# Opening the main attention's buffers at the end of the leading attention, with decoding level with it in the queues

## The chip, the cores and the metric

The kernel runs on one core of one Trainium2 chip. Its time is the device time of an execution in microseconds (us), and the median of several executions is compared. The engines are TensorE (PE), ScalarE (ACT), VectorE (DVE), GpSimd (POOL) and SyncE (SP), which here issues every transfer. Each takes its instructions strictly in the order in which the program was written down, and waits for the semaphores of the others.

## The reference

Attention with a top-32 mask, then a gated MLP, then a mixture of eight experts whose weights P come from a softmax that is normalised over tokens and experts in turn:

```python
scores = scale * np.matmul(q, k.transpose(0, 1, 3, 2))          # q, k, v: (4, 8, 576, 64)
kth = np.partition(scores, -top_k, axis=-1)[..., -top_k:-top_k + 1]
scores = np.where(scores >= kth, scores, -1000000000.0)
attn = np.exp(scores - np.max(scores, axis=-1, keepdims=True))
attn = attn / (np.sum(attn, axis=-1, keepdims=True) + 1e-09)
x = np.matmul(attn, v)                                          # to (2304, 512), heads side by side
h = x @ w_in                                                    # (512, 2048)
x = (h * np.cos(h)) @ w_out                                     # (2048, 512)
P = np.exp(x @ w_gate - (x @ w_gate).max())                     # (2304, 8)
for _ in range(8):
    P /= P.sum(1, keepdims=True) + 1e-09
    P /= P.sum(0, keepdims=True) + 1e-09
    P *= N / E
for e in range(E):
    out += P[:, e:e + 1] * (np.maximum(x @ w1[e], 0.0) @ w2[e]) # (512, 1024), (1024, 512)
```

The weights w_in and w_out reach the kernel as 64-bit floats. They are turned into 32-bit floats on the chip, which the kernel calls decoding.

## The kernel before

There are 18 tiles of 128 tokens. Three of them lead: `attention_tile` does their attention head by head in plain fp32 (24 head tiles, the leading attention, class "first attention"), and `moe1_tile_a` and `moe1_tile_b` their MLP ("first mlp"), so that the first three tiles of x are there early. From them `fill` can compute expert products (L373 to L375), which keep TensorE busy while the rest of the attention ("attention", the main attention, L448 and L449 for QK) and of the MLP runs. The fill begins when the last x2fh and x2fl of the third leading tile are written.

Every head tile of either attention runs through `att_tile`: QK in two halves of 288 columns (L452 plain, L448 and L449 split into two parts), copies to sc (L458), four MAX8 and three MATCH_REPLACE8 on VectorE for the 32 largest (L460 to L464), two small steps on GpSimd (L465, L469) around two ScalarE passes (L466, L467), a reciprocal (L470), the scaling on GpSimd (L471), five transposes (L476), and a product with v (AV: L531 leading, L502 and L504 main). The leading tiles end with a copy to x_f (L535).

Decoding works through 32 blocks of 128x512 numbers, 16 of w_in and 16 of w_out. Each block has a 512 KB load to d_raw, one VectorE operation (L326), four on ScalarE (L327 to L330), GpSimd's L331, VectorE's L332, GpSimd's L333 and L334, and a 256 KB store to win_d or wout_d in DRAM. The buffers d_raw, d_mag, d_sgn (four each) and d_low (five) are of the pool "dec". The leading MLP loads its weights back from there, 512 KB at a time, to the four buffers wp, 48 times, for L632 (first product) and L657 (second). The gate between them is L591 and L592 on GpSimd, L593 and L598 on VectorE, L594 and L595 on ScalarE, and eight transposes (L641).

What sets the order is the class `Plan`. Every operation is recorded with an engine, an assumed cost and its dependencies; `issue` then plays the engines forward in time and, whenever an engine is free, gives it the operation with the lowest (rank, number of recording) among those that are ready. The ranks are the table `PRIORITY`, a row for each engine and a column for each of the five classes. The order found so is written down, and the hardware follows it whatever the real times are. Decoding is recorded before everything else, so that at equal rank it goes ahead of the leading attention.

Pools of buffers share memory by time: a pool with `after` opens when the pools named there are done, and each operation that touches it depends on all operations that touched those. The main attention's buffers (kh, kl, qs, qt, vs, ath, atl) are of the pool "att", which opens after "dec"; the fill's (whi, wlo, gh, gl, xh, xl) are of "fl", which opens after "first". The leading attention's kp, vp, qp and at_f are of "first", beside the x_f, wp and gT of the leading MLP.

Of the kernel before, what the change touches and what calls it, by code (L numbers as in the profile page):

```python
# [10 lines left out]
F32 = mybir.dt.float32  # L11
# [7 lines left out]
DRAM = bass.MemoryType.DRAM  # L19
# [7 lines left out]

CLASSES = ("first attention", "first mlp", "decode", "attention", "mlp")
PRIORITY = {
    "PE": (0, 1, 9, 2, 3),  # L30
    "ACT": (0, 0.5, 1, 2, 1.5),
    "DVE": (1, 0, 0.5, 2, 0),
    "POOL": (0, 0.5, 1, 1.5, 2),
    "SP": (0, 1, 0.5, 2, 3),
}


# [34 lines left out]
class Plan:  # L72
# [15 lines left out]
    def buf(self, pool, shape, dtype, name):  # L88
        return Buf(self, pool, shape, dtype, name)
# [141 lines left out]
def fused_kernel(tc, kq, vv, w_in, w_out, w_gate, w1, w2, out, B=4):  # L231
# [3 lines left out]
    nc = tc.nc  # L235
    V, A_, G_, T_ = nc.vector, nc.scalar, nc.gpsimd, nc.tensor
    H, S, D = 8, 576, 64
# [11 lines left out]
    wide = w_in.dtype == mybir.dt.int64  # L249

    pl = Plan(tc, {
        "dram": dict(space=DRAM), "cst": {}, "mlp": {}, "m1": {}, "ph1": {}, "att": dict(after=("dec",)),
        "ph2": dict(after=("att", "ph1")),
        "first": dict(side="right"), "dec": dict(side="right"), "fl": dict(side="right", after=("first",)),
        "psum": dict(space=PSUM),
    })
    for p in ("dram", "cst", "mlp", "m1", "ph1", "psum", "first", "dec"):
        pl.open(p)
    add, buf = pl.add, pl.buf

# [42 lines left out]
    def ring_of(pool, n, shape, dtype, name):  # L303
        return Cycle([buf(pool, shape, dtype, f"{name}{i}") for i in range(n)])
# [100 lines left out]
    wk_r = ring_of("ph1", 2, [128, S], F32, "wk")  # L405
    ex_r = ring_of("ph1", 3, [128, S], F32, "ex")
    m_r = ring_of("ph1", 4, [128, 40], F32, "m")
    kp_r = ring_of("first", 2, [64, 2, S], F32, "kp")
    vp_r = ring_of("first", 2, [128, 2, 5, D], F32, "vp")
    qp_r = ring_of("first", 2, [64, H, 128], F32, "qp")  # L410
    at_r = ring_of("first", 2, [128, 5, 128], F32, "at_f")
    xf_r = ring_of("first", 2, [128, 4, 128], F32, "x_f")
    wp_r = ring_of("first", 4, [128, 2, 512], F32, "wp")
    gT_r = ring_of("first", 2, [128, NF1, 128], F32, "gT")
# [683 lines left out]
```

## Time and profile before

| | us |
|---|---|
| median of 3 runs | 2428.88 |
| the runs | 2426.16 to 2429.28 |
| the profiled execution | 2435.11 |
| its span, first to last instruction | 2433.3 |
| TensorE busy in the span | 2344.6 (96%) |
| VectorE busy | 1835.7 (75%) |
| ScalarE busy | 1370.4 (56%) |
| GpSimd busy | 1285.8 (53%) |

The page of the profile gives busy shares of the whole span, in which stages with quite different limits are mixed. The views used below look closer: the stretches give busy time by engine in a window, the lines of one source line its count with its first and last start, the timeline single instructions in order of time, with the idle time just before one and what ended it in brackets. In a timeline a row can hold several equal instructions ("x4"), and the time is then from the start of the first to the end of the last. Instructions overlap a little with the next, so the price of one in a dense stretch is the distance from its start to the start of the next.

### The profile page before, as it was taken

The page shows a single profiled execution, that of the slowest core. Times are in us where ns is not written, and L with a number is a line of the kernel's source. Part 1 is how long each engine was busy: PE and PEld are TensorE (multiplying, and loading weights), DVE is VectorE, ACT ScalarE, POOL GpSimd, SP SyncE. Part 2 cuts the span into 40 slices and gives each one's busy share as a digit, 9 for nine tenths or more (in the row PEclk, how much of TensorE's full clock was granted, in tenths as well). Part 3 has the DMA queues.
Part 4 walks back from the last instruction along what each step waited for, and adds up shares of the span by engine and source line. Part 5 has one row for each costly group of instructions (what it writes and reads, how often), then busy time and mean ns, then how long its engine had stood idle before and what let it go on. Part 6 is the DMA issues. An engine that isn't in the chain of part 4 may idle for free.

```text
span 2433.3 us, 33804 instructions
## 1 busy us (share of the span) xinstructions
PE 2344.6 (96%) x11161; PEld 1909.7 (78%) x11161; DVE 1835.7 (75%) x3371; ACT 1370.4 (56%) x2754; POOL 1285.8 (53%) x1352
## 2 busy tenths in 40 slices
PE   7885899999999999999999999999999999999999
PEld 3442489888877888888888898888888888888887
DVE  8883599999997999998156887876667666666555
ACT  7885488888888777777366766322222232222221
POOL 6768388779888666665421045433333344444440
PEclk9887999999999999999999999999999999999999
DMA  8656654555533334333344333122222221111101
GB/s 273 205 163 219 215 179 147 150 163 182 150 99 100 96 117 121 120 99 108 113 131 115 96 111 103 42 75 83 74 74 74 74 63 42 41 38 35 35 22 48
DMA packets 162449, 267.44 MB, mean 110 GB/s; under 512 B 15392, under 2 KB 62576, under 8 KB 162272
## 3 DMA queue, kind: packets, MB, share of 16 engines
q1 hardware_dynamic: 162272, 265.27, 36.1%
q8 instruction: 88, 1.44, 0.3%
q14 instruction: 89, 0.73, 0.1%
HBM read 233.34 MB, written 31.87 MB: 109 GB/s over the span
## 4 chain that ended last, share of the span: by engine, by line
PE 77%; DVE 10%; POOL 5%; ACT 3%; DMA 3%; issue 2%; SPq 0%; POOLq 0%; ACTq 0%; DVEq 0%
PE y L373 11%; PE y L374 11%; PE y L375 11%; PE g L375 3%; PE g L374 3%; PE g L373 3%; PE t L476 2%; DVE wk L463 2%; PE h L373 2%; PE h L374 2%; PE h L375 2%; DVE m L464 2%; PE t L502 1%; PE y L385 1%; PE y L384 1%
## 5 line engine op out<-in xcount | busy, mean ns | idle before, releaser
L348 POOL TENSOR_TENSOR wlo<-raw,whi 128x512 fp32r<-128x512 f32 x336 | 448.6, 1340 | 144.6 <-ACT whi L346 110.2
L464 DVE MAX8 m<-wk 128x8 f32<-128x576 f32 x432 | 317.4, 748 | 2.8
L956 DVE SCALAR_TENSOR_TENSOR acc<-y,P,acc 128x512 f32<-128x512 f32 x308 | 228.6, 747 | 99.6 <-PE y L375 99.4
L346 ACT ACTIVATE whi<-raw 128x512 fp32r<-128x512 f32 x416 | 258.4, 626 | 64.4 <-PE y L375 25.4
L463 DVE MATCH_REPLACE8 wk<-m,wk 128x576 f32<-128x576 f32 x288 | 213.9, 743 | 1.8
L373 PE MATMUL y<-whi,gh 128*128 128x512 f32 x448 | 182.6, 408 | 0.0
L375 PE MATMUL y<-whi,gl 128*128 128x512 f32 x448 | 176.4, 394 | 0.0
L373 PE MATMUL y<-gh,xh 128*128 128x512 f32 x450 | 176.2, 392 | 0.1
L374 PE MATMUL y<-wlo,gh 128*128 128x512 f32 x448 | 175.9, 393 | 0.0
L374 PE MATMUL y<-gl,xh 128*128 128x512 f32 x450 | 175.6, 390 | 0.0
L375 PE MATMUL y<-gh,xl 128*128 128x512 f32 x450 | 175.5, 390 | 0.0
L476 PE MATMUL t<-ident,ex 128*128 128x128 f32 (+1 forms) x720 | 133.9, 286 | 22.8 <-ACT at_f L480 6.8
L476 PEld LDWEIGHTS t<-ident,ex 128*128 128x128 f32 (+1 forms) x720 | 87.8, 140 | 72.3 <-issue 14.5
L458 ACT ACTIVATE sc<-s 128x288 f32<-128x288 f32 x288 | 116.5, 405 | 26.0 <-PE s L449 12.9
L471 POOL TENSOR_SCALAR ex<-ex,m 128x576 f32<-128x576 f32 x144 | 110.4, 767 | 39.2 <-DVE m L470 32.6
L466 ACT ACTIVATE ex<-sc,m 128x576 f32<-128x576 f32 x144 | 111.0, 771 | 33.1 <-DVE m L464 32.9
L494 ACT ACTIVATE ath<-t 64x128 fp32r<-64x128 f32 (+3 forms) x272 | 104.5, 395 | 31.3 <-PE t L476 29.1
L460 DVE MAX8 m<-sc 128x8 f32<-128x576 f32 x144 | 107.2, 745 | 17.8 <-ACT sc L458 17.8
L467 ACT ACTIVATE ex<-ex,m 128x576 f32<-128x576 f32 x144 | 111.2, 772 | 5.5 <-POOL m L465 2.3
L463 DVE MATCH_REPLACE8 wk<-m,sc 128x576 f32<-128x576 f32 x144 | 106.7, 741 | 0.2
L373 PEld LDWEIGHTS y<-gh,xh 128*128 128x128 f32 x450 | 84.5, 188 | 19.0 <-DVE acc L952 0.7
L373 PE MATMUL y<-gh,gh 128*128 128x512 f32 x254 | 99.3, 391 | 0.0
(376 smaller groups left out, 7096.2 us busy)
## 6 DMA issues: line engine op xcount, KB each, us to landing
raw<-in_w_dram SPq DMA_DIRECT2D x384, 256.0 KB, 2.6
kq<-in_kq_dram SPq DMA_DIRECT2D x40, 576.0 KB, 4.2
raw<-win_d SPq DMA_DIRECT2D x64, 256.0 KB, 3.0
raw<-wout_d SPq DMA_DIRECT2D x64, 256.0 KB, 2.7
y_d<-st SPq DMA_DIRECT2D x56, 256.0 KB, 3.1
raw<-y_d SPq DMA_DIRECT2D x56, 256.0 KB, 2.7
wp<-win_d SPq DMA_DIRECT2D x24, 512.0 KB, 4.6
wp<-wout_d SPq DMA_DIRECT2D x24, 512.0 KB, 4.4
```

The lines of the kernel that those rows point to most:

```text
L346: put("ACT", act_ns(n), lambda: A_.activation(hv(), rv(), AF.Copy), [rb], [hb])
L348: put(e, c, lambda: f.tensor_tensor(lv(), rv(), hv().bitcast(F32), op=ALU.subtract), [rb, hb], [lb])
L373: T_.matmul(o(), ah(), bh(), start=start, stop=False)
L374: T_.matmul(o(), ah(), bl(), start=False, stop=False)
L375: T_.matmul(o(), al(), bh(), start=False, stop=stop)
L458: put("ACT", act_ns(288, psum=True), lambda c=c: A_.activation(sc.ap[:, c], o(), AF.Copy), [ps_s], [(sc, c.start, c.stop)])
L463: put("DVE", 669, lambda r=r, src=src: V.match_replace(wk.ap, mc(8 * r, 8), src.ap, LOWEST), [src, (m, 8 * r, 8 * r + 8)], [wk])
L464: put("DVE", 669, lambda r=r: V.max(mc(8 * r + 8, 8), wk.ap), [wk], [(m, 8 * r + 8, 8 * r + 16)])
L466: put("ACT", act_ns(S, ap=True), lambda: A_.activation(ex.ap, sc.ap, AF.Prelu, scale=-1.0, bias=mc(31), alpha=TINY), [sc, (m, 24, 32)], [ex])
L467: put("ACT", act_ns(S, ap=True) + 93.0, lambda: A_.activation(ex.ap, ex.ap, AF.Exp, scale=-0.125 / TINY, bias=mc(32), accum_out=mc(33)), [ ...
L476: T_.transpose(pt()[:p, c - c0, :], ex.ap[:, c * 128 : c * 128 + p], ident.ap)
L956: put("DVE", 663, lambda y=y, av=av, pcol=pcol: V.scalar_tensor_tensor(av(), y.ap, pcol(), av(), op0=ALU.mult, op1=ALU.add), [y, P, a], [a])
```

## The change

The ranks of decoding become 0 on ScalarE (1 before), VectorE (0.5 before) and SP (0.5 before), so that it goes ahead of the leading attention on all three. Main attention's rank on TensorE goes from 2 to 0.5, ahead of the leading MLP (1) and still behind the leading attention (0). The leading attention's buffers kp, vp, qp and at_f move to a pool of their own, "lead", and the pool "att" opens after "lead" instead of after "dec". The pool "fl" now waits for "dec" as well as for "first". The scratch for DMA descriptors is made smaller, which leaves room for both "att" and "dec".

```diff
 CLASSES = ("first attention", "first mlp", "decode", "attention", "mlp")
 PRIORITY = {
-    "PE": (0, 1, 9, 2, 3),
-    "ACT": (0, 0.5, 1, 2, 1.5),
-    "DVE": (1, 0, 0.5, 2, 0),
+    "PE": (0, 1, 9, 0.5, 3),
+    "ACT": (0, 0.5, 0, 2, 1.5),
+    "DVE": (1, 0, 0, 2, 0),
     "POOL": (0, 0.5, 1, 1.5, 2),
-    "SP": (0, 1, 0.5, 2, 3),
+    "SP": (0, 1, 0, 2, 3),
 }
...
-        "dram": dict(space=DRAM), "cst": {}, "mlp": {}, "m1": {}, "ph1": {}, "att": dict(after=("dec",)),
+        "dram": dict(space=DRAM), "cst": {}, "mlp": {}, "m1": {}, "ph1": {}, "lead": {}, "att": dict(after=("lead",)),
         "ph2": dict(after=("att", "ph1")),
-        "first": dict(side="right"), "dec": dict(side="right"), "fl": dict(side="right", after=("first",)),
+        "first": dict(side="right"), "dec": dict(side="right"), "fl": dict(side="right", after=("dec", "first")),
...
-    for p in ("dram", "cst", "mlp", "m1", "ph1", "psum", "first", "dec"):
+    for p in ("dram", "cst", "mlp", "m1", "ph1", "lead", "psum", "first", "dec"):
...
-    kp_r = ring_of("first", 2, [64, 2, S], F32, "kp")
-    vp_r = ring_of("first", 2, [128, 2, 5, D], F32, "vp")
-    qp_r = ring_of("first", 2, [64, H, 128], F32, "qp")
-    at_r = ring_of("first", 2, [128, 5, 128], F32, "at_f")
+    kp_r = ring_of("lead", 2, [64, 2, S], F32, "kp")
+    vp_r = ring_of("lead", 2, [128, 2, 5, D], F32, "vp")
+    qp_r = ring_of("lead", 2, [64, H, 128], F32, "qp")
+    at_r = ring_of("lead", 2, [128, 5, 128], F32, "at_f")
...
-    nc = bacc.Bacc("TRN2", target_bir_lowering=False, num_devices=1)
+    nc = bacc.Bacc("TRN2", target_bir_lowering=False, num_devices=1, dynamic_dma_scratch_size=1024)
```

Three places show what this does to the queues. The first is the head of SP's queue. Before:

```order
L267 DMA qp_87<-in_kq_dram 64x8x128
L267 DMA kp_95<-in_kq_dram 64x2x576
L267 DMA vp_97<-in_v_dram 128x2x320
L267 DMA kp_99<-in_kq_dram 64x2x576
L267 DMA vp_101<-in_v_dram 128x2x320
L267 DMA qp_103<-in_kq_dram 64x8x128
L267 DMA d_raw_105<-in_w_in_dram 128x1024
L267 DMA d_raw_109<-in_w_in_dram 128x1024
```

and after:

```order
L267 DMA d_raw_90<-in_w_in_dram 128x1024
L267 DMA d_raw_98<-in_w_in_dram 128x1024
L267 DMA d_raw_100<-in_w_in_dram 128x1024
L267 DMA d_raw_102<-in_w_in_dram 128x1024
L267 DMA qp_104<-in_kq_dram 64x8x128
L267 DMA kp_106<-in_kq_dram 64x2x576
L267 DMA vp_108<-in_v_dram 128x2x320
L267 DMA kp_114<-in_kq_dram 64x2x576
```

The first four loads of raw weights have moved from behind the leading attention's first six loads to ahead of them.

The second place is GpSimd's queue around the last block of decoding. Before, L471 of the last leading tile lies eleven blocks further up, and the last block is followed by the splitting of k and q for the main attention:

```order
L334 TENSOR_TENSOR d_low_275<-d_mag_158,d_low_275 128x512
L333 TENSOR_TENSOR d_low_148<-d_low_148,d_sgn_184 128x512
L331 TENSOR_TENSOR d_mag_181<-d_mag_181,d_sgn_221 128x512
L334 TENSOR_TENSOR d_low_148<-d_mag_171,d_low_148 128x512
L333 TENSOR_TENSOR d_low_169<-d_low_169,d_sgn_221 128x512
L334 TENSOR_TENSOR d_low_169<-d_mag_181,d_low_169 128x512
L348 TENSOR_TENSOR kl_1446<-kq_117,kh_1441 128x576
L432 TENSOR_TENSOR qs_1444<-kq_117,qs_1444 64x128
```

After, the last block stands between the thirteenth and the fourteenth leading tile (L465, L469 and L471 are one tile's three steps):

```order
L469 TENSOR_SCALAR m_199<-m_199 128x1
L334 TENSOR_TENSOR d_low_191<-d_mag_122,d_low_191 128x512
L471 TENSOR_SCALAR ex_249<-ex_249,m_199 128x576
L333 TENSOR_TENSOR d_low_116<-d_low_116,d_sgn_149 128x512
L331 TENSOR_TENSOR d_mag_147<-d_mag_147,d_sgn_169 128x512
L334 TENSOR_TENSOR d_low_116<-d_mag_136,d_low_116 128x512
L333 TENSOR_TENSOR d_low_132<-d_low_132,d_sgn_169 128x512
L465 TENSOR_SCALAR m_225<-m_225 128x1
L334 TENSOR_TENSOR d_low_132<-d_mag_147,d_low_132 128x512
L469 TENSOR_SCALAR m_225<-m_225 128x1
L471 TENSOR_SCALAR ex_322<-ex_322,m_225 128x576
L465 TENSOR_SCALAR m_247<-m_247 128x1
```

The whole of decoding has moved ahead of eleven of the 24 leading tiles.

The third place is TensorE's queue behind the last AV of the leading attention. Before:

```order
L531 MATMUL t<-at_f_301,vp_101 64x128 x5
L657 MATMUL y_1137<-wp_435,gT_753 128x512 x2
L657 MATMUL y_1137<-wp_515,gT_753 128x512 x2
L657 MATMUL y_1137<-wp_307,gT_753 128x512 x2
L632 MATMUL h<-wp_307,x_f_285 128x512
L657 MATMUL y_1137<-wp_369,gT_753 128x512 x2
```

and after, behind the logits (L605, L606) of the first leading tile:

```order
L632 MATMUL h<-wp_298,x_f_354 128x512
L632 MATMUL y_426<-wp_329,x_f_354 128x512 x2
L448 MATMUL s<-kh_1458,qs_1465 128x288
L449 MATMUL s<-kl_1467,qs_1465 128x288
L632 MATMUL y_426<-wp_386,x_f_354 128x512
L448 MATMUL s<-kh_1458,qs_1465 128x288
L449 MATMUL s<-kl_1467,qs_1465 128x288
```

The second product of the first leading tile (L657 with its gT) is done there already, and main attention's first QK follows the last AV closely. From that AV to the first L373, before has 20 QK matmuls of main attention, 14 transposes and no AV of it, and after has 52, 30 and 18; of the 48 first-MLP matmuls of each kind there remain 16 of L632 and 44 of L657 before, and 13 and 32 after.

## Rows read from the trace of the kernel before

**Rows 1.** Stretches: window, length, busy us (instructions) of PE, PEld, DVE, ACT, POOL; PEclk, DMA share, GB/s.

```profile
0.00:100.00 100.00, 79.71 (x234) 39.85 (x234) 84.64 (x175) 75.64 (x157) 70.85 (x84) 0.93 0.81 251
100.00:200.00 100.00, 82.11 (x324) 45.45 (x323) 77.33 (x161) 90.03 (x177) 67.50 (x76) 0.81 0.56 171
200.00:300.00 100.00, 73.51 (x220) 33.92 (x218) 40.49 (x64) 45.04 (x87) 53.53 (x55) 0.92 0.67 224
...
900.00:1000.00 100.00, 99.78 (x522) 83.09 (x521) 98.23 (x219) 77.17 (x176) 64.04 (x84) 1.00 0.39 116
```

**Rows 2.** Stretches of 20 us, the one behind the leading attention.

```profile
200.00:220.00 20.00, 11.31 (x18) 3.87 (x16) 8.64 (x10) 13.19 (x21) 18.11 (x15) 0.69 0.60 207
```

**Rows 3.** Single lines: duration in ns (min/median/max), first and last start in us, form.

```profile
L535 ACT ACTIVATE x_f<-t x24: 254/268/279, 32.3 to 202.7; 64x128 f32<-64x128 f32 x24
L334 POOL TENSOR_TENSOR d_low<-d_mag,d_low x32: 1257/1268/2298, 19.3 to 231.6; 128x512 f32<-128x512 f32 x32
L332 DVE TENSOR_SCALAR d_sgn<-d_mag x32: 403/787/1486, 17.1 to 228.7; 128x512 int32<-128x512 int32 x32
L373 PE MATMUL g<-x2fh,whi x16: 333/337/420, 298.2 to 337.2; 128*128 128x384 f32 x16
```

**Rows 4.** Timeline of POOL in the decoding tail: start us, us, instruction, idle before.

```profile
209.52 1.38 POOL L333 TENSOR_TENSOR d_low<-d_low,d_sgn 128x512 f32<-128x512 f32 x1 [0.36 <-DVE d_sgn L332]
210.86 1.26 POOL L331 TENSOR_TENSOR d_mag<-d_mag,d_sgn 128x512 f32<-128x512 f32 x1
212.09 1.26 POOL L334 TENSOR_TENSOR d_low<-d_mag,d_low 128x512 f32<-128x512 f32 x1
213.78 1.31 POOL L333 TENSOR_TENSOR d_low<-d_low,d_sgn 128x512 f32<-128x512 f32 x1 [0.43 <-DVE d_sgn L332]
```

**Rows 5.** Timeline of DVE at the same time.

```profile
212.16 1.48 DVE L332 TENSOR_SCALAR d_sgn<-d_mag 128x512 int32<-128x512 int32 x1 [2.38 <-POOL d_mag L331]
```

**Rows 6.** Lines of POOL, first 300 us: count, busy us, mean ns, idle before.

```profile
L471 POOL TENSOR_SCALAR ex<-ex,m 128x576 f32<-128x576 f32 x27 | 21.7, 803 | 5.5 <-DVE m L470 4.9 <-PE t L531 0.5
...
L469 POOL TENSOR_SCALAR m<-m 128x1 f32<-128x1 f32 x27 | 8.0, 297 | 29.0 <-ACT ex L467 27.6
L592 POOL TENSOR_SCALAR rr<-tt 128x1024 f32<-128x1024 f32 x6 | 6.6, 1096 | 0.5
```

**Rows 7.** Timeline of DVE in a dense stretch of the leading attention.

```profile
34.63 0.08 DVE L463 MATCH_VALUE_LOAD wk<-m,wk 128x8 f32 x1
...
35.36 1.41 DVE L464 MAX8 m<-wk 128x8 f32<-128x576 f32 x2
36.69 0.91 DVE L332 TENSOR_SCALAR d_sgn<-d_mag 128x512 int32<-128x512 int32 x1
```

**Rows 8.** Timeline of PE, leading attention and first MLP together, at full clock.

```profile
138.39 0.75 PE L452 MATMUL s<-kp,qp 64*128 64x288 f32 x2
139.06 1.13 PE L632 MATMUL h<-wp,x_f 128*128 128x512 f32 x2
140.03 0.60 PE L476 MATMUL t<-ident,ex 128*128 128x128 f32 x4
140.47 1.02 PE L632 MATMUL h<-wp,x_f 128*128 128x512 f32 x2
...
143.19 1.45 PE L531 MATMUL t<-at_f,vp 128*64 128x128 f32 x10
...
169.18 1.13 PE L657 MATMUL y<-wp,gT 128*128 128x512 f32 x2
```

**Rows 9.** Timeline of PE between the end of decoding and the fill.

```profile
266.21 5.32 PE L657 MATMUL y<-wp,gT 128*128 128x512 f32 x12
...
276.72 0.30 PE L448 MATMUL s<-kh,qt 128*128 128x288 f32 x1
276.85 0.29 PE L449 MATMUL s<-kl,qt 128*128 128x288 f32 x1
```

**Rows 10.** PE's waits in the first 300 us: in total, times, longest.

```profile
PE y L657 <- DMA wp<-wout_d: 15.4, 6, 6.4
```

## The prediction

> **What bounds the kernel now.** I read the stretches first, then the start of the kernel queue by queue. In the first three hundreds of microseconds TensorE idles 20.3, 17.9 and 26.5 us, 65 us in all, and its granted clock is below full there; later it is full, as between 900 and 1000 us [rows 1]. So TensorE is the engine that the end waits for, and the change is priced in one place: the time F at which the expert fill begins on TensorE (its first matmul at 298.2 us [rows 3]), and how much main attention TensorE has done by then. A microsecond off F, or a microsecond of attention done before F, is a microsecond off the end.
>
> Three things end before F. The leading attention ends at A = 203 us, with the last x_f; decoding ends at D = 233 us, with the last L334 [rows 3]. Then the rest of the first MLP and the opening tiles of main attention take 65 us. Between A and D the kernel does little but decode: TensorE is busy 11.3 of 20 us at 0.69 of its clock, VectorE 8.6 of 20 [rows 2]. There GpSimd's three passes over a block are the chain, and L333 to L333 is 4.26 us [rows 4].
>
> **The change part by part.** What moves is decoding, to the front of SP, ScalarE and VectorE, and main attention, which may open at A and not at D.
>
> *Decoding.* On GpSimd the order now puts all 32 blocks ahead of the fourteenth leading tile; before, all 24 tiles stood ahead of the last block. GpSimd's own work up to there is 32 blocks at 4.26 us [rows 4], 136 us; 13 leading tiles with L471 at 0.80 us, L469 at 0.30 and L465, taken like L469, some 1.4 us each, 18 us; and two pairs of gate steps (L591, L592) at 1.1 us an operation, 4 us [rows 6]. The first block can't reach GpSimd before its load and its activations; before, the first L334 began at 19.3 us behind six other transfers [rows 3], now the load leads, and I take 10 us. Together D = 10 + 136 + 18 + 4 = 168, taken as 170 us: 63 us earlier. The bounds: with no gap between GpSimd's passes (1.23 us each from start to start [rows 4], 3.7 a block) D is 150; with a VectorE that is late each time it is 186, worked out under the rivals.
>
> VectorE has room for this. A leading tile costs it four MAX8 and three MATCH_REPLACE8: 1.33 us for two MAX8, 0.73 for a replace with its load [rows 7], 4.9 us in all with the reciprocal. Up to D it has 13.5 tiles, 66 us, and 64 decode operations at 0.40 us at best and 0.79 in the median of L332 [rows 3], at most 50 us in that measure: 116 of 160 us. ScalarE was busy 166 of the first 200 us [rows 1] with 24 leading tiles and most of the decoding; up to D it has 12 tiles and all the decoding, so it isn't the limit either. What is given up is the leading attention: 14 tiles by 170 us instead of about 19 (the 24 copies to x_f start between 32.3 and 202.7 [rows 3]). On SP four 512 KB loads of raw weights stand ahead of the first q, k and v. That delays the first leading tile by a few microseconds, which cost nothing while GpSimd sets the pace; without that cover they would be paid in full.
>
> *From D to F.* Now TensorE and VectorE are scarce. From the fourteenth AV to F the new order gives TensorE: 13 QK halves at 0.67 us (start to start), 10 AVs at 1.45, 50 transposes at 0.11 (four of them 0.44) [rows 8]; 28 matmuls of L632 and 48 of L657, each two instructions, at 0.88 (5.32 us for twelve instructions), and 52 QK matmuls of main attention at 0.13 [rows 9]; 30 more transposes, 18 AV matmuls and some 70 small ones at about 0.1. That is 8.7 + 14.5 + 5.5 + 66.9 + 6.8 + 3.3 + 2.3 + 7 = 115 us. VectorE has 10.5 leading and about 7.5 main tiles at 4.9 us, 88 us, and four gates beside them: close behind, not ahead. How dense can TensorE run with such a mix? Between 138.4 and 169.2 us it ran leading tiles and first-MLP matmuls together (the first of 122 instructions and the one after the last stand in [rows 8]): 4 AVs, 8 QK halves, 30 MLP instructions, 20 transposes and 16 of the gate are 28 us of work in 30.8, or 0.92. I take that: 115 / 0.92 = 125 us, and 3 us from GpSimd's last block to the fourteenth AV. F = 170 + 3 + 125 = 298 us, where it was before: what decoding gives, the later leading attention takes.
>
> *What F then holds.* Main attention is further on at F: 52 QK matmuls instead of 20, 30 transposes instead of 14, 18 AV matmuls instead of none. At the same prices that is 4.2 + 1.8 + 2.3 = 8 us of TensorE's time, and it is taken out of a stretch where TensorE is full.
>
> *The rest.* Against the fill, main attention keeps its rank on TensorE; only against the first MLP is the rank turned round, and that is in the order counted above. The smaller scratch for DMA touches no transfer of this profile, all of which SP issues; I cost it at nothing. The fill's buffers now wait for the end of decoding too, which is long past when they open.
>
> **The sum.** 0 + 8 = 8 us off. The profiled execution had a span of 2433.3 and 2435.1 us in all, 6.2 above the median of the runs, 2428.9. So the span becomes about 2425 and the median 2421 us, 0.3% less.
>
> **The rivals.** *About even.* The same order, but TensorE at 0.87 between D and F, because VectorE is loaded to 0.8 beside it and all queues are strictly in order. The stretch takes 132 us, F is 305, and 8 - 7 = 1 us remains: 2428. Anything from 0.84 to 0.90 ends within 5 us of no change. For it speaks that two engines are so full at once; against it the 0.92 that the trace shows.
>
> *Slower: VectorE and GpSimd lock each other.* A decode TENSOR_SCALAR that starts while GpSimd is in a pass takes as long as the pass: 1.48 us beside the L334 that started 0.07 us earlier [rows 4, 5], against 0.40 alone [rows 3]. With GpSimd busy nearly all the time, each of the 64 may meet a pass. At 1.48 us they cost 95 us; with 66 for the tiles VectorE has 161 in a phase of 160, and GpSimd in turn waits for d_sgn. At 0.92 of that, D is 10 + 161 / 0.92 = 185, F is 185 + 128 = 313, 15 us later, less the 8: 7 us slower, 2436. It decides once the mean of L326 and L332 passes 1.2 us. The Trainium skill, "SBUF — State Buffer", section "Who interferes with whom", says that a VectorE instruction in a two-port mode and a GpSimd one exclude each other for the whole instruction, and that whoever issues first wins. By that rule the whole price is due each time GpSimd is ahead; the trace agrees in the 1.48 us, and the median of 0.79 shows that over the whole decoding it was due only part of the time.
>
> *Slower: the wp stream.* All loads go through SP in order, and in the new order the last wp loads stand behind loads of kq, which wait for GpSimd's kl, and behind stores of x_d, which wait for VectorE. If these hold TensorE once more as long as its six waits for wp did before, 15.4 us [rows 10], F is 313 and the kernel again 7 us slower, 2436.
>
> *Not what it says.* If main attention never waited for D but for other engines, opening it earlier brings nothing and the reordering is neutral: 2429. The engines stood idle, not loaded, between A and D [rows 2], so I give this little.
>
> **How the numbers follow.** Forecast 0.42, even 0.26, locked engines 0.20, the wp stream 0.08, not what it says 0.04. A measurement of this kernel can tell some 0.2% (5 us) from no change. So faster 0.42, same 0.30, slower 0.28. The forecast's own range is 2406 to 2424. The whole range takes in D from 158 to 186 and a density of 0.82 to 0.96: with D = 158 and 0.96 F is 281 and the gain 25; with 186 and 0.87 F is 321 and the loss 15. That is 2404 to 2444.
>
> **What would show it.** Right: the last L334 ends near 170 us, the last x_f near 235, the first L373 between 290 and 302; TensorE nearly without idle time from 170 us on, and the stretches from 800 us on as before. The locked engines show as L326 and L332 with means above 1.2 us and a last L334 past 182; the wp stream as waits of L657 of 15 us after the last x_f; the even case as a TensorE that works at under 0.9 between D and F with neither. The forecast is wrong if decoding ends on time and F is still past 305, or if the stretch from F to 800 us, which I take as unchanged, moves by more than 5 us.

## The result and the profile after

The changed kernel takes 2444.5 us (median of 4 executions, 2444.3 to 2447.3) against 2428.7 (2426.2 to 2429.3): ratio 1.0061, 95% interval 1.0041 to 1.0081. It is 15.8 us slower. The forecast was 2421 us, faster; the direction is wrong, and the time lies half a microsecond above the range. The profiled execution of after has a span of 2442.5 us and took 2444.3, its median; that of before lies 6 us above its own, so between the two profiles only 9 of the 16 us can be seen.

The stretches of after that answer to [rows 1], with the columns explained there, and the one from 700 to 800 us:

```profile
0.00:100.00 100.00, 49.55 (x121) 24.27 (x121) 67.76 (x126) 75.43 (x143) 81.91 (x83) 0.86 0.87 274
100.00:200.00 100.00, 83.91 (x262) 42.63 (x260) 88.77 (x160) 72.15 (x143) 72.76 (x76) 0.71 0.49 151
200.00:300.00 100.00, 97.90 (x408) 52.27 (x408) 70.74 (x147) 72.89 (x153) 41.58 (x63) 1.00 0.69 223
...
700.00:800.00 100.00, 85.56 (x390) 68.47 (x389) 83.20 (x122) 81.29 (x135) 77.11 (x66) 0.97 0.29 82
```

The first 100 us hold 49.6 us of TensorE work where they held 79.7; from 200 to 300 us TensorE is now full at full clock, where it worked 73.5. The work has moved behind decoding. The single lines that answer to [rows 3], and VectorE's other decode line:

```profile
L535 ACT ACTIVATE x_f<-t x24: 252/269/272, 50.3 to 250.1; 64x128 f32<-64x128 f32 x24
L334 POOL TENSOR_TENSOR d_low<-d_mag,d_low x32: 1262/1272/1710, 12.8 to 172.3; 128x512 f32<-128x512 f32 x32
L332 DVE TENSOR_SCALAR d_sgn<-d_mag x32: 407/746/1503, 9.7 to 168.8; 128x512 int32<-128x512 int32 x32
L326 DVE TENSOR_SCALAR d_mag<-d_raw x32: 408/520/1496, 4.6 to 150.3; 128x512 int32<-128x512 int32 x32
L373 PE MATMUL g<-x2fh,whi x16: 336/338/522, 314.0 to 351.9; 128*128 128x384 f32 x16
```

Decoding ends at D = 173.5 us (before 232.8), the leading attention at A = 250.3 (202.9), and the fill begins at F = 314.0 (298.2). What TensorE waits for in the first 100 us of after (in total, times, longest):

```profile
PE s L452 <- ACT sc L458: 16.6, 12, 3.2
PE s L452 <- DMA kp<-in_kq_dram: 11.9, 1, 11.9
PE t L476 <- POOL ex L471: 10.8, 3, 4.8
```

and the same of before:

```profile
PE s L452 <- DMA kp<-in_kq_dram: 6.3, 1, 6.3
PE s L452 <- ACT sc L458: 5.5, 7, 1.3
...
PE t L476 <- POOL ex L471: 2.4, 2, 2.2
```

TensorE waits longer for ScalarE's copies, for GpSimd's L471 and for the first loads. (On GpSimd the ranks are as before; decoding has moved ahead of the leading tiles on ScalarE, VectorE and SP.) The first x_f is written at 50.5 us, before at 32.5. In return the waits for wp of [rows 10] are gone: no wait of L657 for wp is left between 200 and 325 us.

**A count that explains the time.** I add up what TensorE loses: its idle time, and half of its busy time where the granted clock is 0.5, the lower of its two levels. (Ahead of the first clock record, some 59 us in before and 69 in after, I take the lower level, since the pairs of L452 show 1.32 us there and 0.75 at the higher one.) Such a pair in before:

```profile
25.65 1.32 PE L452 MATMUL s<-kp,qp 64*128 64x288 f32 x2
```

Span less loss is 2288 to 2295 us in all sixteen profiles here that run the reference's work and no more, whose spans lie between 2416 and 2446 us. So the loss is most of the difference between them; between before and after it grows by 13.4 us and the span by 9.2. Loss up to a time, in us:

```
                        100 us  200 us   at F   behind F   F      work done at F
before                   48.5    81.1   113.7     26.1    298.2       184.5
after                    74.6   117.0   123.2     30.0    314.0       190.9
first 16 blocks ahead    70.9    94.9   102.1     22.9    294.9       192.9
last 16 blocks ahead     48.5    93.3   106.6     21.2    301.9       195.3
```

(The two last kernels are experiments below.) Before loses 33 us between 200 us and F, in the tail of decoding and behind it; after loses 6 there. But by 200 us it has lost 36 more. The change trades a loss behind the leading attention for a larger one during decoding: 36 us more ahead of 200 us against 27 less between there and F.

### The profile page after: what moved, and what is told of

It reads as the page before. It is cut to its first block, busy times and chain, and to the rows that moved or that the text cites. A ratio compares the mean times of both kernels' runs of the same rounds, so it can differ in the third digit from the quotient of the medians.

```text
span 2442.5 us, 33847 instructions
## 1 busy us (share of the span) xinstructions
PE 2347.7 (96%) x11161; PEld 1914.4 (78%) x11161; DVE 1850.1 (76%) x3371; ACT 1377.6 (56%) x2756; POOL 1286.5 (53%) x1352
## 4 chain that ended last, share of the span: by engine, by line
PE 83%; DVE 8%; POOL 4%; ACT 2%; DMA 2%; issue 1%; POOLq 0%; DVEq 0%; ACTq 0%
PE y L373 11%; PE y L375 11%; PE y L374 11%; PE g L373 4%; PE g L374 4%; PE g L375 4%; PE t L476 3%; PE h L373 3%; PE h L374 3%; PE h L375 3%; DVE wk L463 2%; PE t L502 2%; PE y L388 1%; DVE m L464 1%; PE y L384 1%
## 5 line engine op out<-in xcount | busy, mean ns | idle before, releaser
L464 DVE MAX8 m<-wk 128x8 f32<-128x576 f32 x432 | 317.9, 749 | 3.5
L373 PE MATMUL y<-whi,gh 128*128 128x512 f32 x448 | 181.8, 406 | 0.0
L373 PE MATMUL y<-gh,xh 128*128 128x512 f32 x450 | 176.1, 391 | 0.1
L476 PE MATMUL t<-ident,ex 128*128 128x128 f32 (+1 forms) x720 | 134.7, 287 | 32.4 <-POOL ex L471 13.3
L458 ACT ACTIVATE sc<-s 128x288 f32<-128x288 f32 x288 | 116.5, 404 | 29.4 <-PE s L449 15.7
L471 POOL TENSOR_SCALAR ex<-ex,m 128x576 f32<-128x576 f32 x144 | 110.8, 770 | 38.3 <-DVE m L470 35.0
L466 ACT ACTIVATE ex<-sc,m 128x576 f32<-128x576 f32 x144 | 110.9, 771 | 20.9 <-DVE m L464 20.7
L460 DVE MAX8 m<-sc 128x8 f32<-128x576 f32 x144 | 107.6, 747 | 12.9 <-ACT sc L458 12.7
L373 PEld LDWEIGHTS y<-gh,xh 128*128 128x128 f32 x450 | 84.5, 188 | 19.1 <-DVE acc L952 0.8
L373 PE MATMUL y<-gh,gh 128*128 128x512 f32 x254 | 99.2, 391 | 0.0
```

The costliest lines, as they stand in the source:

```text
L373: T_.matmul(o(), ah(), bh(), start=start, stop=False)
L458: put("ACT", act_ns(288, psum=True), lambda c=c: A_.activation(sc.ap[:, c], o(), AF.Copy), [ps_s], [(sc, c.start, c.stop)])
L464: put("DVE", 669, lambda r=r: V.max(mc(8 * r + 8, 8), wk.ap), [wk], [(m, 8 * r + 8, 8 * r + 16)])
L466: put("ACT", act_ns(S, ap=True), lambda: A_.activation(ex.ap, sc.ap, AF.Prelu, scale=-1.0, bias=mc(31), alpha=TINY), [sc, (m, 24, 32)], [ex])
L476: T_.transpose(pt()[:p, c - c0, :], ex.ap[:, c * 128 : c * 128 + p], ident.ap)
```

## The experiments

The times are medians; ratios are to the kernel before on the same chip, with their 95% intervals. D, A, F and the losses come from the profiled execution of each, which lies up to 8 us above the median of its kernel (the last row; 6 in before), so a few microseconds of loss between two rows mean little.

```
                                   median   ratio (interval)          D    A    F   loss to F  behind F
decoding's ranks alone             2435.9  1.0027 (1.0015 to 1.0039)  176  251  300   121.4     25.0
all but decoding's ranks           2427.8  1.0000 (0.9987 to 1.0014)  227  196  310   107.5     24.3
pools and scratch alone            2429.5  1.0013 (0.9999 to 1.0027)  229  198  296   109.4     24.8
attention's TensorE rank back      2444.0  1.0063 (1.0045 to 1.0082)  173  254  305   126.3     27.9
ScalarE's rank back                2442.0  1.0058 (1.0039 to 1.0077)  234  217  325   122.9     28.4
VectorE's rank back                2444.3  1.0076 (1.0051 to 1.0101)  176  253  316   125.1     26.2
transfer queue's rank back         2446.6  1.0083 (1.0062 to 1.0104)  184  254  320   130.4     24.7
before, once more                  2429.1  1.0008 (0.9996 to 1.0019)  233  203  298   112.4     25.9
first 16 blocks ahead              2420.5  0.9967 (0.9954 to 0.9981)  196  232  295   102.1     22.9
last 16 blocks ahead               2418.0  0.9964 (0.9949 to 0.9979)  217  227  302   106.6     21.2
last 8 blocks ahead                2441.5  1.0051 (1.0034 to 1.0067)  229  204  322   117.9     32.3
last 24 blocks ahead               2432.3  1.0017 (1.0004 to 1.0031)  201  243  308   116.0     28.9
first 8 blocks ahead               2421.3  0.9965 (0.9950 to 0.9980)  226  211  303   104.5     27.6
last 16 ahead, pools of before     2417.0  0.9945 (0.9928 to 0.9961)  223  233  287   108.5     23.4
```

### Ranks or pools

Theory 1 was that decoding's ranks starve the leading attention; theory 2 that the cost is in main attention's earlier opening and its rank. Decoding's ranks alone, in the kernel before:

```diff
-    "ACT": (0, 0.5, 1, 2, 1.5),
-    "DVE": (1, 0, 0.5, 2, 0),
+    "ACT": (0, 0.5, 0, 2, 1.5),
+    "DVE": (1, 0, 0, 2, 0),
-    "SP": (0, 1, 0.5, 2, 3),
+    "SP": (0, 1, 0, 2, 3),
```

> The kernel before with only the three decoding ranks of the change (ScalarE, VectorE and the transfer queue at 0); pools, attention's TensorE rank and scratch as before. Theory 1 (decoding's rank starves the leading attention, which then has to be done by a TensorE at its lower clock and as the bound): last decoding tile near 173 us, last x_f 235 to 255 instead of 203, first fill matmul 305 to 315 instead of 298, time 2436 to 2446 us. Theory 2 (the early opening of main attention's buffers and its TensorE rank 0.5 cost the time): last decoding tile near 173, first fill matmul at or before 298, time 2420 to 2430.

The time met theory 1 at its low end, but F stayed at 300: only 3 of the 26 main QK halves that after has done by F are done here. The changed kernel with these three rows put back, everything else as changed:

```diff
-    "ACT": (0, 0.5, 0, 2, 1.5),
-    "DVE": (1, 0, 0, 2, 0),
+    "ACT": (0, 0.5, 1, 2, 1.5),
+    "DVE": (1, 0, 0.5, 2, 0),
-    "SP": (0, 1, 0, 2, 3),
+    "SP": (0, 1, 0.5, 2, 3),
```

> The changed kernel with the three decoding ranks put back (ScalarE 1, VectorE 0.5, queue 0.5); the lead pool, the opening of main attention's buffers at its end, rank 0.5 of attention on TensorE and the scratch stay. Theory 1: last decoding tile near 233, last x_f near 203, main attention starts near 205 on engines that would idle, first fill matmul 293 to 300 with more of main attention done ahead of it than before; time 2412 to 2428 us. Theory 2: the time stays with the change, 2438 to 2446.

D and A came as theory 1 said, and the time is that of before, at the end of what it allowed; F was missed (310), because far more of main attention now stands ahead of it. With attention's TensorE rank back too:

```diff
-    "PE": (0, 1, 9, 0.5, 3),
+    "PE": (0, 1, 9, 2, 3),
```

> As the run without the decoding ranks, and attention's TensorE rank back at 2 too: only the pools and the scratch are changed. Theory 1: within 5 us of the run without the ranks, 2412 to 2430 us. Theory 2, if the cost is in the rank 0.5: 2425 to 2430; if in the early opening: 2438 to 2446.

This time lies in the ranges of both theories; it is the run before that speaks against theory 2.

And the changed kernel with that one row put back, decoding's ranks as changed:

> The changed kernel with attention's TensorE rank put back to 2; decoding ranks and pools as changed. Theory 1: last x_f and first fill matmul stay late (245 to 255, 305 to 316), time 2436 to 2447 us. Theory 2, if the cost is that main attention goes ahead of the first MLP on TensorE: first fill matmul 290 to 302, time 2420 to 2430.

Theory 1 is met, with A at 254, F at 305 and 2444.0 us. Rank 0.5 on TensorE moves F by 9 to 14 us and the time by less than can be told. So the pools alone cost nothing measurable (1.0013), decoding's ranks alone 7.7 us, both together 15.8. The ranks carry the cost; that it doubles with the pools is not explained by these four. The count only places the other 8 us: 5 of them are lost ahead of F and 3 behind it (146.4 us in all with the ranks alone, 154.2 with ranks and pools).

### One rank at a time

Each of the next three is the changed kernel with one of decoding's ranks put back:

```diff
-    "ACT": (0, 0.5, 0, 2, 1.5),
+    "ACT": (0, 0.5, 1, 2, 1.5),
```

> The changed kernel with ScalarE's rank for decoding put back to 1 (VectorE and transfer queue stay at 0, pools as changed). If ScalarE's rank is what starves the leading attention: last decoding tile 195 to 235 us, last x_f 203 to 220, time 2425 to 2434 us. If another of the three does it: last x_f 240 to 255, time 2440 to 2447.

```diff
-    "DVE": (1, 0, 0, 2, 0),
+    "DVE": (1, 0, 0.5, 2, 0),
```

> The changed kernel with VectorE's rank for decoding put back to 0.5 (the others stay at 0). The leading attention has rank 1 there either way, so only the first MLP and the later MLP work change places with decoding: last x_f 245 to 254 and 2440 to 2447 us if ScalarE's or the queue's rank is the cause; 2425 to 2434 if VectorE's is.

```diff
-    "SP": (0, 1, 0, 2, 3),
+    "SP": (0, 1, 0.5, 2, 3),
```

> The changed kernel with the transfer queue's rank for decoding put back to 0.5 (ScalarE and VectorE stay at 0). The leading tiles' loads then go ahead of decoding's again: first leading QK matmul near 6.3 us instead of 11.9. If the queue starves the leading attention: last x_f 203 to 225, time 2425 to 2434 us. If ScalarE's rank does: last x_f 235 to 250, time 2436 to 2446.

None of them is the one cause, and VectorE's rank changes nothing, as forecast for the case that another rank is the cause. Without ScalarE's rank A comes back to 217 and D goes back to 234, as if it were the cause, and the time is still 2442: the queue's rank alone brings the leading loads late (first wait for kp 13.3 us), and the tail of decoding is no shorter. A fits the alternative of ScalarE's rank, the time that of the other two. Without the queue's rank the first QK starts at 6.3 us, but A stays at 254 and the time at 2446.6 us, both late by a little even for the second alternative: ScalarE holds the tiles back. TensorE's waits for it in the first 100 us are

```profile
PE s L452 <- ACT sc L458: 18.2, 9, 9.6
PE t L476 <- ACT at_f L480: 16.5, 4, 11.8
```

A late A alone therefore doesn't explain the time, which is against theory 1 as I had put it.

### Is it TensorE's clock?

Around D the granted clock is low (0.50 from 171 to 186 us in after), and the fourteenth leading tile, which I had put 3 us behind D, ends its AV 11 us behind it. Rows of TensorE there in after:

```profile
175.81 1.33 PE L452 MATMUL s<-kp,qp 64*128 64x288 f32 x2 [0.50 <-ACT sc L458]
177.64 1.32 PE L452 MATMUL s<-kp,qp 64*128 64x288 f32 x2 [0.50 <-ACT sc L458]
...
181.97 2.58 PE L531 MATMUL t<-at_f,vp 128*64 128x128 f32 x10 [0.36 <-ACT at_f L480]
```

against 0.75 and 1.45 us in [rows 8]. To tell whether the clock costs the time, unused 128x128 matmuls were put into TensorE's own order wherever the trace of after shows a wait there, and nothing else was moved:

```diff
+        fill, seen = {0: 23, 1: 4, 2: 6, ..., 87: 4, 88: 1}, 0
         for k in order:
+            if ops[k].eng == "PE":
+                for _ in range(fill.get(seen, 0)):
+                    self.spin()
+                seen += 1
             ops[k].emit()
...
+    pl.spin = lambda: T_.matmul(ps_g.ap[:, 0:128], ident.ap, ident.ap, start=True, stop=True)
```

> The changed kernel in its own order, with 99 extra 128x128 matmuls on TensorE (results unused) put where TensorE waits over 0.65 us before 176 us in the trace of after; no other engine gets anything more. If the lower granted clock around the end of decoding (168 to 195 us, some 10 us of TensorE time between there and the last x_f) is a cause: the QK halves there take 0.7 instead of 1.25 us, last x_f 238 to 244, first fill matmul 302 to 309, time 2432 to 2440 us. If the clock there only goes with it and the order of the work sets the end: last x_f 250 or later, time 2444 to 2450.

It took 2447.1 us, 1.0081 (1.0057 to 1.0105), with A at 250.8 and F at 313.7, as expected if the clock isn't the cause. TensorE's idle time up to D fell from 65 to 35 us, but the clock fell at 165 us all the same, where TensorE still waits 2.7 us. So that run did not yet separate the two. With more of them between 125 and 184 us:

```diff
-        fill, seen = {..., 58: 1, ..., 66: 1, 80: 1, 81: 1, 87: 4, 88: 1}, 0
+        fill, seen = {..., 58: 7, ..., 66: 5, 69: 2, 78: 5, 80: 6, 81: 3, 87: 14, 88: 2, 95: 2, 96: 2, 100: 2}, 0
```

> The run with the waits filled, and 41 more unused 128x128 matmuls ahead of the 11 operations that TensorE still waited for between 125 and 184 us there, 10 of them ahead of the transpose that waits 2.7 us at 165.5. If TensorE then stays at its higher clock through 165 to 195 and the clock is what costs the leading tiles their time: last x_f 240 to 246, first fill matmul 303 to 310, time 2433 to 2440 us. If the clock is not what sets the end there: last x_f and time within 3 us of the run before it (250, 2447).

It took 2442.6 us, 1.0056 (1.0040 to 1.0073), with A at 250.4: the last x_f is where the second alternative puts it, the time, 4 us under the run before, fits neither. Its lines L458, L464 and L537 are L452, L458 and L531 of after; TensorE's rows there, and the stretch from 171 to 186 us in this kernel:

```profile
173.85 0.75 PE L458 MATMUL s<-kp,qp 64*128 64x288 f32 x2 [1.12 <-ACT sc L464]
...
176.33 0.75 PE L458 MATMUL s<-kp,qp 64*128 64x288 f32 x2 [1.08 <-ACT sc L464]
...
182.04 2.59 PE L537 MATMUL t<-at_f,vp 128*64 128x128 f32 x10
```

```profile
171.00:186.00 15.00, 12.54 (x48) 7.44 (x48) 14.86 (x32) 8.16 (x19) 5.60 (x10) 0.75 0.24 73
```

and the same stretch of after:

```profile
171.00:186.00 15.00, 13.64 (x36) 7.34 (x37) 14.46 (x30) 8.61 (x19) 4.98 (x9) 0.50 0.18 54
```

The QK halves take 0.75 us up to 178 us, and the fourteenth AV still starts at 182.04, where it started at 181.97. The faster matmuls waited longer for sc, 1.1 us instead of 0.5. But this run is also 1.1 us late by then: GpSimd's L471 of the fourteenth tile starts at 176.89 instead of 175.76. So the tile takes 1.1 us less from the end of L471 to its AV when the clock is high up to 178 us, not the same time.

VectorE is nearly full in this stretch, in either kernel: 14.5 and 14.9 of 15 us, on the MAX8 and MATCH_REPLACE8 of several leading tiles. It is hardly what the fourteenth tile waits for, though. Rows of that tile in after, with the last block of decoding:

```profile
171.61 0.78 ACT L466 ACTIVATE ex<-sc,m 128x576 f32<-128x576 f32 x1 [0.40 <-DVE m L464]
172.27 1.27 POOL L334 TENSOR_TENSOR d_low<-d_mag,d_low 128x512 f32<-128x512 f32 x1
175.76 0.74 POOL L471 TENSOR_SCALAR ex<-ex,m 128x576 f32<-128x576 f32 x1 [0.62 <-DVE m L470]
178.89 1.11 PE L476 MATMUL t<-ident,ex 128*128 128x128 f32 x4
179.94 1.32 PE L452 MATMUL s<-kp,qp 64*128 64x288 f32 x2
```

Its last MAX8 released L466 at 171.6, ahead of D. L471 ends at 176.5, 3.0 us behind D, and from there to the end of the AV it takes 8.0 us. That is nothing unusual: from the end of an L471 to the end of its AV the 24 tiles of before take 5.6 to 12.7 us, 9.1 in the median. The shortest of them, at the higher clock:

```profile
67.71 0.75 POOL L471 TENSOR_SCALAR ex<-ex,m 128x576 f32<-128x576 f32 x1 [0.53 <-PE t L531]
72.59 1.45 PE L531 MATMUL t<-at_f,vp 128*64 128x128 f32 x10
```

In TensorE's order other tiles' work stands between L471 and the AV; in after these are the QK halves at 175.81, 177.64 and 179.94.

What the lower clock costs behind 178 us was not told apart: from there to 195 us it was low in both kernels. The stretch of after around it:

```profile
180.00:200.00 20.00, 19.44 (x59) 9.82 (x58) 17.12 (x39) 9.81 (x25) 3.65 (x9) 0.61 0.15 38
```

TensorE is busier there than VectorE, 19.4 us against 17.1, at a granted clock of 0.61. From 178.9 to 196 us it idles 0.4 us, and by the count above it loses 8.1 us to the lower clock. So, as an estimate from these numbers, up to 8 us of the later F can be the clock's; no run here held the clock up in that stretch, and this cause stays open.

### How many blocks ahead

If starving the first leading tiles were the whole cause, raising the ranks for the first half of the blocks should keep the cost. For these runs decoding has two classes, one with the ranks of before and one with rank 0 on ScalarE, VectorE and the queue; the pools are as changed:

```diff
-    "ACT": (0, 0.5, 0, 2, 1.5),
+    "ACT": (0, 0.5, 0, 2, 1.5, 1),
...
     for f in range(NF1):
+        work = "decode w_out"
         fresh(w_out[f], ...)
```

> The changed kernel with decoding's ranks at 0 only for the first 16 tiles (w_in); the last 16 (w_out) have the ranks of before. If what costs the time is that leading tiles are kept from TensorE at the start, nearly all of the cost stays: TensorE's idle and lower-clock time up to the first fill matmul 118 to 128 us (123 in the changed kernel, 108 without the ranks), time 2438 to 2446 us. If it is the end of decoding that matters: 2426 to 2434.

The other way round:

```diff
-    "ACT": (0, 0.5, 0, 2, 1.5),
+    "ACT": (0, 0.5, 1, 2, 1.5, 0),
```

> The changed kernel with decoding's ranks at 0 only for the last 16 tiles (w_out); the first 16 (w_in) have the ranks of before. Starvation at the start: first leading QK matmul at 6, first six x_f as before (32 to 68 us), TensorE's idle and lower-clock time up to the first fill matmul 100 to 114 us, time 2420 to 2432 us. If the end of decoding matters: 2438 to 2446.

The second came as starvation at the start says (first x_f at 32.6 us, a loss of 106.6), and at 2418.0 us 2 us better than its range. The first refutes theory 1 in its simple form: with the first 16 blocks ahead the leading attention starts exactly as late as in after (first x_f at 50.5 us in both, loss at 100 us 70.9 and 74.6), and the kernel is faster than before. Its 2420.5 us lies under both alternatives. The stretches of the kernel with the first half ahead:

```profile
0.00:100.00 100.00, 52.97 (x131) 25.53 (x132) 72.39 (x135) 74.12 (x145) 79.51 (x82) 0.88 0.86 276
100.00:200.00 100.00, 87.61 (x328) 45.07 (x328) 92.53 (x189) 86.82 (x173) 80.69 (x90) 0.88 0.61 182
200.00:300.00 100.00, 92.69 (x391) 51.12 (x389) 70.37 (x145) 70.35 (x153) 47.64 (x68) 0.98 0.64 213
```

Beside after, it is the second hundred that differs: ScalarE works 86.8 us there instead of 72.2, VectorE 92.5 instead of 88.8, and TensorE runs 87.6 us at 0.88 instead of 83.9 at 0.71. In after ScalarE has done with decoding by 152 us and is busy only 9.8 of 20 us between 180 and 200, while TensorE, at its lower clock for most of that, and VectorE are nearly full. With half of the blocks behind the tiles D comes 22 us later than in after, at 196, and A 18 us earlier, at 232.

Theory 3, then, is a trade: while decoding goes ahead, TensorE loses leading work; what comes back is the loss in decoding's tail. By it the best is in between. Four more runs, three with the class set at another block and one with the pools of before; the edit of the second (last 24) is:

```diff
+            work = "decode first" if b * 4 + c >= 8 else "decode"
             fresh(w_in[c, b], ...)
     for f in range(NF1):
+        work = "decode first"
         fresh(w_out[f], ...)
```

> Decoding's ranks at 0 for the last 8 of the 32 tiles, the ranks of before for the others; pools as changed. Theory of a trade (decoding's rank takes TensorE's leading work from it for as long as it holds, and gives back TensorE's waits at the end of decoding): TensorE's loss up to the first fill matmul (idle, and half of the busy time at the lower clock) between that without the ranks (108 us) and that with the last 16 (104), time 2417 to 2428 us. Rival (any rank of 0 costs in proportion to the tiles that have it): 2430 to 2434.

> Decoding's ranks at 0 for the last 24 of the 32 tiles. Trade: the loss grows from that of the last 16 (104 us) toward that of all 32 (123), loss 108 to 118 us, time 2422 to 2438. Rival (only the first tiles' rank costs, since there the first leading tiles wait for their loads; without it the gain stays): loss 100 to 106 us, time 2412 to 2420.

> Decoding's ranks at 0 for the first 8 of the 32 tiles only; pools as changed. Trade: first leading QK matmul at 12 us, loss at 100 us 55 to 68 (49 before, 71 with the first 16), end of decoding 205 to 225 us, loss up to the first fill matmul 102 to 112, time 2416 to 2428 us. Rival (the late start of the leading tiles is never made up): loss 113 to 125 us, time 2430 to 2442.

Last 24 and first 8 came as the trade says (loss 116 and 104.5, 2432 and 2421 us; first 8 with its first QK 1 us and its D half a microsecond past what was expected); the rival of the first tiles fell, since the last 24 leave the start alone (first x_f at 33.0) and lose more than the last 16. Last 8 met neither theory: 2441.5 us, loss 118 instead of 104 to 108. Its leading attention and its decoding end nearly as without the ranks (204 and 229 us, there 196 and 227), but between 260 and 280 us TensorE works 13.2 of 20 us at 0.88, waiting in turn for GpSimd (3.0), wp of L657 (2.0) and wp of L632 (1.3), and behind F it loses 32.3 us, 8 more than the kernel without the ranks. The kernel without ScalarE's rank has its low stretch at the same place. I have no cause for it that a run shows: each set of ranks gives `issue` another order, and that order is part of the result. So the theory of a trade doesn't hold for every order, and the time is not a smooth curve of the number of blocks: 2427.8, 2441.5, 2418.0, 2432.3 and 2444.5 us for 0, 8, 16, 24 and 32 blocks from the end.

> The kernel before (its pools, scratch and attention's TensorE rank) with decoding's ranks at 0 for the last 16 tiles. Decoding then ends near 217 us and opens main attention's buffers itself. If the gain of the half-way ranks is in TensorE's loss alone: loss up to the first fill matmul 100 to 110 us, time 2418 to 2426. If the early opening is what makes it a gain: 2426 to 2434.

This is the kernel before with the two classes of the last 16 and nothing else. It came as expected if the gain is in TensorE's loss alone (108.5 us; the time is 1 us better than that range, and D is 6 us later than expected). At 2417.0 us, 0.9945 (0.9928 to 0.9961), it is faster than before and than the change. So the gain does not need the pools of the change, nor main attention's earlier opening.

### The profile of before

> The kernel before, unchanged, for a second profile: its first one was 6 us above its median. Median 2426 to 2430 us; if the 6 us lay in TensorE's waits after the first fill matmul (17 us between 300 and 800 us) those are 8 to 13 us here and the first fill matmul stays at 298; if they lay before it, the first fill matmul comes at 291 to 296.

The profiled execution again took 2435 us, 6 above its median, with F at 297.5 and the same idle time between F and 800 us (16.4 us, before 17.1). Neither place was it; where a median execution of before saves these 6 us stays open.

## Why the prediction was wrong, point by point

**What bounds the kernel: right.** TensorE sets the end, and F with the work done by then is the right place to price. What TensorE loses before D (65 us idle in after, against 38 up to A in before) is not missing from the forecast: the leading work that isn't done by D stands in its 115 us behind D, and so it had F unchanged, at 298 us. F came 16 us later than that: 3.5 us are D's own, 8 lie between D and the fourteenth AV, and 4.5 behind it.

**Decoding: nearly right.** D was to be 170 and is 173.5, and 13 tiles were done then (x_f of the thirteenth at 171.2). The first leading QK starts 5.6 us later, the few microseconds forecast; but the first x_f comes 18 us later, so these microseconds were not all that decoding's loads and steps cost the first tile.

**The first step that failed: 3 us from D to the fourteenth AV.** It ends at 184.5, 11.0 us behind D. The tile's L471 ends 3.0 us behind D, which alone uses up the 3 us, and from there to the end of the AV it takes another 8.0. The trace of before had the price: 5.6 us at least, 9.1 in the median. In these 11 us TensorE idles 1.4 us; 4.8 are work at full clock, with four QK halves of other tiles in it, and 4.8 are lost to the lower clock. With 11 in place of 3 the forecast's own sum gives F = 306 and, with the 8 us off, a time as before.

**The second, smaller: 115 us of work at a density of 0.92.** From there to F it took 129.5 us instead of 125: 117.7 of work, 5.5 idle and 6.3 lost to the lower clock, where I had priced all of it at the full one. VectorE was not far behind, as forecast, and TensorE hardly idled. From D to F the lower clock takes 11.1 us and idle time 6.8; how much earlier F would be at full clock, no run shows. Together F = 173.5 + 11 + 129.5 = 314, where I had 170 + 3 + 125 = 298. That A came at 250 and not 235 is the same error seen from the leading attention; F - A is 64 us, 63 in the forecast.

**The 8 us of main attention: right.** At F it is exactly as far as counted (26 QK halves, 30 transposes, 10 + 8 AV matmuls). In the count of TensorE's work this is 6.4 us.

**From F to the end: nearly right.** 2128.5 us in the profile, 2127 forecast. Inside it 700 to 800 us lost 7 us (85.6 us of work instead of 92.5) and 300 to 700 gained about 5, so the bound of 5 us that I had set for the sum holds, and the stretches behind 800 us are as before.

**From span to median.** I took 6 us off the span, since before's profile lay that much above its median. The profile of after lies on its own. That is 6 of the 23 us between 2421 and 2444; the 16 at F are most of the others.

**The rivals.** The locked engines did not come: L332 has a mean of 0.86 us and L326 of 0.79, both under the 1.2 that would decide it, and D is nearly on time. The Trainium skill, "SBUF — State Buffer", section "Who interferes with whom", which this rival went by, fits the 1.50 us of the slowest ones; 17 of the 64 took over 1.2 us. The wp stream did not come either (1.1 us of waits for wp up to 315 us).

The even case had the right place, the stretch behind D. By the prediction's own prices the density there was 115 / 129.5 = 0.89, between its 0.87 and the forecast's 0.92. Its reason, VectorE's load, is not shown: TensorE idled 5.5 us there and lost 6.3 to its clock. It had the 3 us behind D unchanged, so its F of 305 is still 9 us short.

The trade between the two streams stood in the forecast, as break-even ("what decoding gives, the later leading attention takes"). What I lacked is a rival in which the stretch right behind D runs slower than priced: leading tiles at 5.6 us or more from L471 to AV, and a TensorE below its full clock, as it is in [rows 2].

## What to carry to other kernels

When two streams share the engines ahead of a bottleneck, going first and going last are not the only orders to price: what counts is the bottleneck's lost time up to the point where both have ended. Here all blocks behind cost 114 us, all ahead 123, half ahead 102 to 107. So sum the idle and low-clock time of the bottleneck up to one later point for each order, and look for an order between the two; but measure it, since the last 8 blocks ahead cost 118 us without a cause that I can show.

And a step of the new order that looks like a small remainder should be read from the old trace: 3 us stood in the sum for a passage whose last part alone, from L471 to the end of the AV, took 5.6 to 12.7 us in the 24 tiles of before.

## What the runs showed of the hardware that I had not expected

Filling part of TensorE's waits did not keep its clock up. With the second set of unused matmuls it was busy 14.9 of 20 us between 20 and 40 us, and the granted clock of that stretch was 0.62:

```profile
20.00:40.00 20.00, 14.91 (x49) 9.84 (x47) 17.95 (x36) 12.67 (x25) 16.31 (x15) 0.62 0.94 327
```

And ten microseconds at the higher clock moved no later x_f: from 168 to 178 us the QK halves went from 1.33 to 0.75 us, and from the thirteenth x_f on (171.2 us) none moved by more than 0.2 us, in a run that was 1.1 us behind at GpSimd's L471. The waits for sc grew from 0.5 to 1.1 us there.
